# Gated attention and spatial mixer on one core: all four spatial chunks ahead of all sixteen output row tiles

## The chip, the cores and the metric

One core of a Trainium2 chip runs the whole kernel. The metric is the device time in microseconds (us). TensorE (PE) multiplies matrices into eight banks of PSUM, VectorE (DVE) and ScalarE (ACT) work on tiles of SBUF and read the banks, GpSimd (POOL) does almost nothing here, and SyncE (SP) issues most of the DMA transfers, in the order in which they are written; some are issued by ACT's queue. An engine works through its own queue in order.

## The reference

`x` is 2048 x 1024, bf16. The result is `g*a + (1-g)*b` with a gate `g` for each row.

```python
g = sigmoid((x * gate_w).sum(-1))
# a: attention over 8 earlier positions, 2 apart, 32 heads of 32
q, k, v = split(x @ wqkv)
o = softmax(q . k[pos - 2w] * scale) . v[pos - 2w]
a = o @ wo
# b: gated mixer, Fh = 1792
z = gelu(x @ w_in)                       # 2048 x 3584
z1, z2 = z[:, :Fh], layernorm(z[:, Fh:])
u = z1 * (w_sp @ z2 + b_sp[:, None])     # w_sp is 2048 x 2048
b = u @ w_out                            # 1792 x 1024
```

## The kernel before

The 2048 positions make 16 row tiles of 128; the 1792 columns of `z2` make 14 tiles f. All of SBUF's working space is one tile, `arena`, cut by hand into regions (Z for `z2`, X for the transposed `x`, A for the attention, CD and EF for what comes and goes); a region is used again by a later stage. Instructions keep the order in which the code issues them (`manual_schedule`), each engine in its own queue; the tile framework adds the waits. `Beat` (from L207) is the planner: `beat.run` advances a clock by the matmuls issued, `beat.at(t, fn)` issues `fn` when the clock passes `t`, and the steps of the attention, which DVE does, are issued between the matmuls of the stages that PE is in. So where a DVE step lands among the others follows from planned times, and where DVE runs behind the plan, the queue just gets later.

The stages on PE, in order: the second half of `z` (L279), `wqkv` (L501), the rest of `z2` (L279), `z1` (L538), which goes to DRAM, and then the spatial product, `w_sp @ z2`, in four chunks of 512 positions.

- Chunks 0 and 1 (`g_chunk`, L552) are 14 x 16 matmuls each. ACT copies each bank out (L556), DVE adds the bias and multiplies by `z1` (L557, L558), into `z1c_slots`.
- `final_chunk(0)` and `final_chunk(1)` make the output rows 0 to 7: for each row and half of the columns 8 matmuls of attention times `wo` (`attn_mm`, L565) and 14 of `u` times `w_out` (`mixer_mm`, L581); ACT scales the one (L588), DVE joins the two (L589).
- Chunks 2 and 3 are one product of 2 x 2 blocks with seven products in place of eight (`seven_products(n)` for n = 0 to 6, L668, 56 matmuls each). It multiplies sums of tiles in fp16: sums of `z2` (`s_sum`, L655 to L661) and sums of the weights (`t_sums`, `t1` to `t4`). The rows of the weights are scaled by powers of two first: they are loaded in natural order (`natural`), summed (`row_sums`, `row_sums_fast`), scaled (`scale_rows`), written to DRAM and loaded again transposed (`load_wsp`). In `seven_products` two banks are added to after they have been read: the last product adds to a bank that L708 (`TT(gsb, pb, e5)`) must have read.
- `late_chunks` makes the output rows 8 to 15 in four pairs. Each pair's mixer is again seven products of seven matmuls (`late_mix`, L828) with sums of `u` (`u_scale` L792, `u_sum` L799 to L805) and of `w_out` (`w_scale` L770, `w_sum` L775 to L781). The powers of two for `w_out` and `u` come from `w_largest` (L755), `u_sums` (L787, on ACT) and `whole_power`: small DVE steps with a transpose and a broadcast on PE between them (L740, L743). Between the last `seven_products` and the first pair stand attention products (`attn_pair(0)` and four halves, L810) and the sums for the pair.

`w_out` is loaded into X as soon as chunk 0 begins (L980). `wo` is loaded into A in two parts (`load_wo`, L417, five and three of its eight tiles; four transfers each), the first at the end of the attention's q and k. Its destination is strided by four partitions:

```python
dst = bass.AP(tensor=wo_sb.tensor, offset=wo_sb.offset + h * pitch + k0 * D,
              ap=[[pitch * HG, DH], [D, k1 - k0], [1, D]])
```

Of the kernel before, what the change touches and what calls it, by code (L numbers as in the profile page):

```python
# [10 lines left out]
F32 = mybir.dt.float32  # L11
# [4 lines left out]
P = 128  # L16
# [39 lines left out]
def kernel(  # L56
# [72 lines left out]
    w_max = sm.tile([P, 4], F32, name="w_max")  # L129
# [6 lines left out]
    u_up = sm.tile([P, 1], I32, name="u_up")  # L136
    back = sm.tile([P, 1], I32, name="back")
# [10 lines left out]
    w_out_sb = reg(X_OFF, NF * D).rearrange("p (f n) -> p f n", f=NF)  # L148
# [5 lines left out]
    wo_sb = reg(A_OFF, KT * D).rearrange("p (k n) -> p k n", k=KT)  # L154
    oT_slots = [reg(A_OFF + 8192 + r * 1024, 1024).rearrange("p (k t) -> p k t", k=KT) for r in range(3)]
    ob_slots = [reg(A_OFF + 11264 + r * 1024, 1024) for r in range(3)]
    asb_slots = [reg(A_OFF + 14336 + r * 1024, 1024).bitcast(F32) for r in range(2)]
# [9 lines left out]
                 reg(EF_OFF, 8192).rearrange("p (i a t) -> p i a t", i=16, a=4)]  # L167
# [5 lines left out]
    nat_slots = [reg(off, S) for off in (X_OFF + NF * D, A_OFF + 16384, A_OFF + 18432, X_OFF + NF * D)]  # L173
    nat_slots += [reg(CD_OFF + k * S, S) for k in range(4)]

    def half16(off, n):
        return reg(off, n * 512).bitcast(F16).rearrange("p (k t) -> p k t", k=n)

    sums = [reg(off, 1024).bitcast(F16).rearrange("p (k q) -> p k q", k=8)
            for off in (CD_OFF + 14336, A_OFF + 20480, EF_OFF + 8192, EF_OFF + 9216)]  # L180
    u_first = reg(EF_OFF + 10240, 2048).rearrange("p (h i q) -> p h i q", h=2, i=8)
    t1 = half16(CD_OFF + 8192, 8)
    t2 = half16(A_OFF + 16384, 8)
    t3 = half16(EF_OFF, 8)
    t4_parts = [half16(X_OFF + NF * D, 4), half16(CD_OFF + 12288, 4)]

    w_sums = reg(Z_OFF, 16 * FH).bitcast(F16).rearrange("p (f i n) -> p f i n", f=NF, i=4)
    late_asb = [reg(CD_OFF + r * 1024, 1024).bitcast(F32) for r in range(8)]
    late_oT = {a: oT_slots[a % 3] for a in (8, 9, 10)}
    for r, a in enumerate((11, 12, 13, 14)):  # L190
        late_oT[a] = reg(CD_OFF + 8192 + r * 1024, 1024).rearrange("p (k t) -> p k t", k=KT)
    late_oT[15] = late_oT[8]
    late_ob = ob_slots + [reg(A_OFF + 14336, 1024)]
    late_e5 = [reg(A_OFF + 16384 + r * 1024, 1024).bitcast(F32) for r in range(2)]
    late_sums = [[reg(EF_OFF + (4 * r + k) * 896, 896).bitcast(F16).rearrange("p (k q) -> p k q", k=7)
                  for k in range(4)] for r in range(2)]
# [179 lines left out]
    def attention_steps(t):  # L376
        beat.at(t - 8.0, lambda: load_qk(0))
        beat.at(t - 7.9, lambda: load_v(0))
        for g in range(NG):
# [3 lines left out]
            if g + 1 < NG:  # L383
                beat.at(t + 1.0, lambda g=g: load_qk(g + 1))
            else:
                beat.at(t + 1.0, lambda: load_wo(0, 5))
# [21 lines left out]
        beat.at(t + 1.5, lambda: load_wo(5, KT))  # L408
        for a in range(3):
            beat.at(t + 8.0, lambda a=a: load_oT(a))  # L410

    def load_wo(k0, k1):
        pitch = wo_sb.ap[0][0]
        for h in range(HG):
            dst = bass.AP(tensor=wo_sb.tensor, offset=wo_sb.offset + h * pitch + k0 * D,
                          ap=[[pitch * HG, DH], [D, k1 - k0], [1, D]])
            sync.dma_start(dst, wo_v[k0:k1, h, :, :].rearrange("g d n -> d g n"))  # L417

    def load_oT(a):
        sync.dma_start_transpose(oT_slots[a % 3], o_d[a * P:(a + 1) * P, :])  # L420
# [26 lines left out]
    def load_wsp(c, aa):  # L447
        src = wsp_v[4 * c + aa] if c < 2 else wsp_d[4 * (c - 2) + aa]
        sync.dma_start_transpose(wsp_slots[c % 2][:, :, aa, :], src)
# [78 lines left out]

    for f in range(NF):
# [16 lines left out]
    def g_chunk(c):  # L546
        wsp = wsp_slots[c % 2]
# [14 lines left out]
    def attn_mm(a, n0, nw):  # L562
        psa = psum.tile([P, 512], F32, name="psa", tag="ps")
        for kt in range(KT):
            nc.tensor.matmul(psa[:, 0:nw], oT_slots[a % 3][:, kt, :], wo_sb[:, kt, n0:n0 + nw],  # L565
                             start=(kt == 0), stop=(kt == KT - 1))
        beat.run(KT * nw)
        return psa

    def u_tile(f, a):  # L570
        if a < 8:
            return z1c_slots[a // 4][:, f, a % 4 * P:(a % 4 + 1) * P]
        return u_late(f)[:, a - 8, :]

    def u_late(f):
        return u_first[:, f // 7] if f % 7 == 0 else z2[:, f - 1, 0:8, :]

    def mixer_mm(a, n0, nw):
        psb = psum.tile([P, 512], F32, name="psb", tag="ps")
        for f in range(NF):  # L580
            nc.tensor.matmul(psb[:, 0:nw], u_tile(f, a), w_out_sb[:, f, n0:n0 + nw],  # L581
                             start=(f == 0), stop=(f == NF - 1))
        beat.run(NF * nw)
        return psb

    def combine(a, n0, nw, slot, psa, psb):
        asb = asb_slots[slot][:, 0:nw]
        nc.scalar.activation(asb, psa[:, 0:nw], ACT.Copy, scale=g_s[:, a:a + 1])  # L588
        nc.vector.scalar_tensor_tensor(ob_slots[a % 3][:, n0:n0 + nw], psb[:, 0:nw], omg[:, a:a + 1], asb,  # L589
                                       ALU.mult, ALU.add)  # L590
# [8 lines left out]
    def row_sums_fast(r):  # L599
        nc.vector.tensor_reduce(l1[:, r, 0:1], nat_slots[r], AX.X, ALU.add, apply_absolute_value=True)  # L600

# [5 lines left out]
    def row_powers(r0, r1, parts):  # L607
        v = nc.vector
        sl = slice(r0, r1)
        v.tensor_reduce(row[:, sl], l1[:, sl, 0:parts], AX.X, ALU.add)  # L610
# [26 lines left out]
    b_lo = wsp_slots[0].rearrange("p i a t -> p i (a t)")  # L637
    b_hi = wsp_slots[1].rearrange("p i a t -> p i (a t)")

    def t_sums(k):  # L640
        if k == 0:
            TT(t1, b_hi[:, 0:8], b_lo[:, 0:8], ALU.subtract)
        elif k == 1:
            TT(t2, b_hi[:, 8:16], t1, ALU.subtract)
        elif k == 2:
            TT(t3, b_hi[:, 8:16], b_hi[:, 0:8], ALU.subtract)
        else:
            h = 4 * (k - 3)
            TT(t4_parts[k - 3], b_lo[:, 8 + h:12 + h], t2[:, h:h + 4], ALU.subtract)
# [29 lines left out]
    def seven_products(n):  # L679
# [5 lines left out]
        e5 = asb_slots[n % 2]  # L685
# [7 lines left out]
        if more:  # L693
            s_sum(n + 1, 0)
        product(pb, sums[1], lambda k: t2[:, k], False)
# [8 lines left out]
        if n:  # L704
            w_scale(n - 1)
# [4 lines left out]
        if n:  # L710
            w_sum(n - 1, 0)
            w_sum(n - 1, 1)
# [6 lines left out]
        if n:  # L719
            w_sum(n - 1, 2)  # L720
            w_sum(n - 1, 3)
        product(pb, z2[:, fb, 8:16, :], lambda k: t4_parts[k // 4][:, k % 4], False)
# [5 lines left out]
        g_out(fb, 2, gsb)  # L728
        beat.run(56 * 512)

    def whole_power(src, up1):
# [18 lines left out]
        v.tensor_scalar(omg[:, 8:16], omg[:, 8:16], back[:].bitcast(F32), None, ALU.mult)  # L750
        yield

    def w_largest(k):
        f0, f1 = (0, 4, 8, 11, 14)[k:k + 2]
        nc.vector.tensor_reduce(w_max[:, k:k + 1], w_out_sb[:, f0:f1, :].rearrange("p f n -> p (f n)"), AX.X, ALU.max,  # L755
                                apply_absolute_value=True)
        if k == 3:
            nc.vector.tensor_reduce(top[:], w_max[:], AX.X, ALU.max)

    def w_tiles(j):  # L760
        f = (j + 1) % 7
# [3 lines left out]
    def w_t(j, k):  # L765
        return w_sums[:, j + 7 * (k // 2), 2 + k % 2, :]

    def w_scale(j):
        for f in ((j + 1) % 7, (j + 1) % 7 + 7):
            nc.vector.tensor_scalar(w_out_sb[:, f, :], w_out_sb[:, f, :], w_up[:].bitcast(F32), None, ALU.mult)  # L770

    def w_sum(j, k):
        b11, b12, b21, b22 = w_tiles(j)
        if k == 0:
            TT(w_t(j, 0), b12, b11, ALU.subtract)  # L775
        elif k == 1:
            TT(w_t(j, 1), b22, w_t(j, 0), ALU.subtract)
        elif k == 2:
            TT(w_t(j, 2), b22, b12, ALU.subtract)
        else:  # L780
            TT(w_t(j, 3), b21, w_t(j, 1), ALU.subtract)  # L781
# [7 lines left out]

    def u_scale(q):  # L790
        v = z2[:, :, 2 * q:2 * q + 2, :]
        nc.vector.tensor_scalar(v, v, u_up[:].bitcast(F32), None, ALU.mult)  # L792

    def u_sum(q, k):
        s = late_sums[q % 2]
        a11, a12 = z2[:, 0:7, 2 * q, :], z2[:, 7:14, 2 * q, :]
        a21, a22 = z2[:, 0:7, 2 * q + 1, :], z2[:, 7:14, 2 * q + 1, :]
# [236 lines left out]
```

## Time and profile before

| | |
|---|---|
| median of 3 runs | 701.32 us (701.2 to 702.38) |
| the profiled execution | 701.97 us, of which the span from first to last instruction is 700.2 us |
| PE busy | 691.3 us, 99% |
| DVE busy | 510.6 us, 73% |
| ACT busy | 306.0 us, 44% |
| POOL busy | 14.0 us, 2% |
| mean granted PE clock | 0.999 |
| HBM read, written | 51.91 MB, 32.57 MB |
| chunks 0 and 1 on PE | 366.6 to 463.5 us of the span |
| rows 0 to 7 | 463.5 to 541.7 us |
| `seven_products` | 541.7 to 626.3 us |
| rows 8 to 15 | 626.3 us to the last matmul's end at 696.5 us |

The stages' bounds are where the chain of waits goes from one line to the next. A matmul's record is longer than the time from one matmul to the next, since they are pipelined: 379 ns against 0.2158 us (768 matmuls of L501 follow each other in 165.76 us). A group of lines names engine, line and operation, what it writes and reads, then busy time and mean, then idle time ahead of it and what ended that.

### The profile page before, as it was taken

What the parts mean: (1) busy time and instruction counts of PE and PEld (TensorE: products, weight loads), DVE (VectorE), ACT (ScalarE), POOL (GpSimd) and SP (SyncE); (2) the same over time, 40 slices, a digit from 0 to 9 for tenths busy, and PEclk for the clock granted to TensorE, in tenths of its full rate; (3) what the DMA queues carried; (4) which work ended last, traced back from release to release, by engine and by line L of the source; (5) the groups of instructions that cost most, each with busy time, mean ns of one, the idle gap of its engine ahead of it and who ended that gap; (6) DMA issues with size and microseconds to landing.
All of it is one profiled execution on the core that took longest, in us unless ns stands there. A gap on an engine that the chain in (4) does not pass through costs nothing.

```text
span 700.2 us, 8520 instructions
## 1 busy us (share of the span) xinstructions
PE 691.3 (99%) x3232; PEld 355.6 (51%) x3281; DVE 510.6 (73%) x596; ACT 306.0 (44%) x576; POOL 14.0 (2%) x23
## 2 busy tenths in 40 slices
PE   8999999999999999999999999999999999999998
PEld 4466666666665554444444444444444444444443
DVE  0000398999999999999999999943496578677452
ACT  4444544435359887344351228533311254554211
POOL 1000000000000211000000000000000000000000
PEclk9999999999999999999999999999999999999999
DMA  9994974976465120994348973199852401130010
GB/s 225 188 192 91 263 170 126 237 175 178 125 168 183 57 102 28 216 315 137 105 147 233 367 233 136 61 294 204 197 131 61 122 30 46 45 62 16 30 61 30
DMA packets 182968, 101.29 MB, mean 145 GB/s; under 512 B 145808, under 2 KB 171408, under 8 KB 182672
## 3 DMA queue, kind: packets, MB, share of 16 engines
q1 hardware_dynamic: 180624, 92.37, 50.0%
q10 hardware_dynamic: 2304, 8.39, 3.3%
q8 instruction: 25, 0.41, 0.2%
q14 instruction: 15, 0.12, 0.1%
HBM read 51.91 MB, written 32.57 MB: 121 GB/s over the span
## 4 chain that ended last, share of the span: by engine, by line
PE 97%; DMA 2%; issue 0%; SPq 0%; DVE 0%; DVEq 0%
PE ps L501 24%; PE ps L552 14%; PE ps L538 14%; PE ps L279 14%; PE ps L668 12%; PE psb L581 7%; PE ps L828 6%; PE psa L810 4%; PE psa L565 3%; DMA arena<-in_B_w_in_dram 1%; DMA arena<-o_d 1%; SPq L459 0%; SPq L457 0%; PE po L743 0%; DVE arena L900 0%
## 5 line engine op out<-in xcount | busy, mean ns | idle before, releaser
L501 PE MATMUL ps<-arena 128*128 128x512 bf16 x768 | 165.9, 379 | 0.0
L501 PEld LDWEIGHTS <-arena 128*128 128x128 bf16 x768 | 110.7, 144 | 55.1
L323 DVE TENSOR_TENSOR arena<-arena 128x8192 bf16<-128x8192 bf16 x16 | 70.8, 4423 | 51.9 <-DMA arena<-k_d 51.6
L279 PE MATMUL ps<-arena 128*128 128x512 bf16 (+1 forms) x501 | 97.5, 353 | 1.7 <-DMA arena<-in_B_w_in_dram 1.1
L552 PE MATMUL ps<-arena 128*128 128x512 bf16 x439 | 96.6, 379 | 0.5
L538 PE MATMUL ps<-arena 128*128 128x512 bf16 x439 | 96.4, 379 | 0.5
L504 ACT CAST arena<-ps 128x512 bf16<-128x512 f32 x96 | 55.7, 587 | 93.2 <-PE ps L501 86.4
L668 PE MATMUL ps<-arena 128*128 128x512 f16 (+1 forms) x385 | 84.4, 379 | 0.4
L326 DVE TENSOR_TENSOR arena<-arena 128x4096 bf16<-128x4096 bf16 (+1 forms) x64 | 77.5, 1210 | 1.9
L279 PEld LDWEIGHTS <-arena 128*128 128x128 bf16 x512 | 50.1, 98 | 48.7 <-issue 2.1
L356 DVE TENSOR_TENSOR arena<-arena,att_A 128x8192 bf16<-128x8192 bf16 x16 | 70.7, 4421 | 0.2
L538 PEld LDWEIGHTS <-arena 128*128 128x128 bf16 x448 | 43.7, 98 | 52.8
L552 PEld LDWEIGHTS <-arena 128*128 128x128 bf16 x448 | 43.6, 98 | 52.8
L668 PEld LDWEIGHTS <-arena 128*128 128x128 bf16 (+1 forms) x392 | 38.3, 98 | 46.3
L540 ACT ACTIVATE arena<-ps 128x512 bf16<-128x512 f32 x56 | 32.3, 597 | 52.0 <-PE ps L538 39.6
L581 PE MATMUL psb<-arena 128*128 128x512 bf16 x220 | 50.0, 379 | 0.3
L284 ACT ACTIVATE arena<-ps 128x512 bf16<-128x512 f32 (+1 forms) x64 | 34.3, 538 | 25.7 <-PE ps L279 25.6
L828 PE MATMUL ps<-arena 128*128 128x512 f16 (+1 forms) x193 | 42.5, 379 | 0.2
L556 ACT CAST arena<-ps 128x512 bf16<-128x512 f32 x28 | 16.3, 582 | 51.7 <-PE ps L552 26.5
L362 DVE TENSOR_TENSOR arena<-arena 128x4096 bf16<-128x4096 bf16 x16 | 36.6, 2290 | 0.4
L588 ACT ACTIVATE arena<-psa,g_s 128x512 f32<-128x512 f32 x16 | 10.9, 686 | 58.3 <-PE psa L565 47.1
L581 PEld LDWEIGHTS <-arena 128*128 128x128 bf16 x224 | 21.7, 98 | 26.3 <-issue 0.2
(142 smaller groups left out, 573.9 us busy)
## 6 DMA issues: line engine op xcount, KB each, us to landing
arena<-k_d SPq DMA_DIRECT2D x8, 960.0 KB, 7.2
arena<-v_d SPq DMA_DIRECT2D x8, 960.0 KB, 5.3
z_d<-arena SPq DMA_DIRECT2D x14, 512.0 KB, 3.7
arena<-in_A_wqkv_dram SPq DMA_DIRECT2D x24, 256.0 KB, 4.4
arena<-in_B_w_in_dram SPq DMA_DIRECT2D x4, 1024.0 KB, 6.0
q_d<-arena SPq DMA_DIRECT2D x32, 128.0 KB, 2.3
k_d<-arena SPq DMA_DIRECT2D x32, 128.0 KB, 2.3
v_d<-arena SPq DMA_DIRECT2D x32, 128.0 KB, 2.4
```

Of the source, the lines that this page charges most:

```text
L279: nc.tensor.matmul(ps[:, 0:N], xT[:, kt, i * P:(i + 1) * P], w2[:, kt, ZC * c:ZC * c + N], start=(kt == 0), stop=(kt == KT - 1))
L323: TT(prod.rearrange("p (w j c) -> p w j c", w=W, j=8, c=C), in0, in1, ALU.mult)
L326: return lambda: TT(pv[:, :, 0:half], pv[:, :, 0:half], pv[:, :, half:2 * half], ALU.add)
L356: TT(prod.rearrange("p (w j d h) -> p w j d h", w=W, j=8, d=DH, h=HG), in0, in1, ALU.mult)
L362: return [(4.4, mul), (2.3, lambda: TT(p3[:, 0:4, :], p3[:, 0:4, :], p3[:, 4:8, :], ALU.add)), (1.2, lambda: TT(p3[:, 0:2, :], p3[:, 0:2, ...
L501: nc.tensor.matmul(ps[:].rearrange("p (t c) -> p t c", t=4), lhsT, wgt[:, :, kt, :], start=(kt == 0), stop=(kt == KT - 1))
L504: nc.scalar.copy(st[:, j % 4, :], ps[:])
L538: nc.tensor.matmul(ps[:], w1[:, kt, (f % 4) * P:(f % 4 + 1) * P], xT[:, kt, 512 * c:512 * (c + 1)], start=(kt == 0), stop=(kt == KT - 1))
L552: nc.tensor.matmul(ps[:], z2[:, f, i, :], wsp[:, i, :, :].rearrange("p a t -> p (a t)"), start=(i == 0), stop=(i == 15))
L581: nc.tensor.matmul(psb[:, 0:nw], u_tile(f, a), w_out_sb[:, f, n0:n0 + nw], start=(f == 0), stop=(f == NF - 1))
L668: nc.tensor.matmul(dst[:], lhs[:, k, :], rhs(k), start=first and k == 0, stop=k == 7, skip_group_check=not first)
L828: nc.tensor.matmul(dst[:], lhs(j), rhs(j), start=first and j == 0, stop=j == 6, skip_group_check=not first)
```

## The change

Chunks 0 and 1 are followed at once by `seven_products`; then all sixteen rows are made in eight pairs. Rows 0 to 7 now use the seven products too.

- `mix_pair(q)` takes the place of `late_mix`, and `attn_pair(q)` follows each `mix_pair`; `attn_mm`, `mixer_mm`, `combine`, `final_chunk`, `late_chunks` and the attention halves ahead of the first pair go. For the first four pairs `u` lies in `z1c_slots` and has a power of its own (`v_sum`, `v_up`), so there is a third `whole_power`.
- All eight row tiles of the weights are loaded by ACT's queue ahead of chunk 0, and summed and scaled (all sums on ACT) at planned times in chunks 0 and 1; `t_sums(0)`, `t_sums(1)` and the first `s_sum`s are issued at the end of chunk 1, `t_sums(2)` and `(3)` in n = 0, since `t2` and `t4` lie where chunk 1's weights were.
- The size of `w_out` is read beforehand: seven loads of two tiles (512 KB each) during `z1`, each summed by ACT. `w_out` itself is loaded in n = 1, into the attention's region A.
- `extra(n, place)` issues, at six places of each n, what goes beside the products: `w_scale` and `w_sum` for one tile in n = 3 and 5 and for two in n = 4 and 6 (before: one tile in each n from 1 on), the power for the first rows in n = 5 and 6, the load of `wo` (one part now, 512 KB in each of four transfers, into CD, where chunk 2's weights were) and the first pair's sums in n = 6.
- The rows of the attention's result are loaded (`load_oT`) into four slots, the first four after n = 6.

```diff
-    w_out_sb = reg(X_OFF, NF * D).rearrange("p (f n) -> p f n", f=NF)
+    w_out_sb = reg(A_OFF + 6144, NF * D).rearrange("p (f n) -> p f n", f=NF)
...
-    wo_sb = reg(A_OFF, KT * D).rearrange("p (k n) -> p k n", k=KT)
+    wo_sb = reg(CD_OFF, KT * D).rearrange("p (k n) -> p k n", k=KT)
...
+    u_first = reg(A_OFF, 2048).rearrange("p (h i q) -> p h i q", h=2, i=8)
+    e5_slots = [reg(A_OFF + 2048 + r * 1024, 1024).bitcast(F32) for r in range(2)]
+    t1 = half16(X_OFF + 8192, 8)
+    t2 = half16(EF_OFF, 8)
+    t3 = half16(X_OFF, 8)
+    t4 = half16(EF_OFF + 4096, 8)
...
+    def load_wo():
         pitch = wo_sb.ap[0][0]
         for h in range(HG):
+            dst = bass.AP(tensor=wo_sb.tensor, offset=wo_sb.offset + h * pitch, ap=[[pitch * HG, DH], [D, KT], [1, D]])
+            sync.dma_start(dst, wo_v[:, h, :, :].rearrange("g d n -> d g n"))
...
+    wout_v = B_w_out.rearrange("(f p) n -> p f n", p=P)
+    for k in range(7):
+        slot = look_slots[k % 2]
+        beat.at(beat.now + 4.0 + 11.0 * k, lambda k=k, slot=slot: sync.dma_start(
+            slot.rearrange("p (f n) -> p f n", f=2), wout_v[:, 2 * k:2 * k + 2, :]))
+        beat.at(beat.now + 14.0 + 11.0 * k, lambda k=k, slot=slot: nc.scalar.activation(
+            look_out, slot, ACT.Abs, accum_out=w_l1[:, k:k + 1]))
...
-    def seven_products(n):
+    def seven_products(n, extra):
...
+        extra(n, 0)
         pa = bank()
         product(pa, z2[:, fa, 0:8, :], lambda k: b_lo[:, k], True)
         pb = bank()
         nc.scalar.copy(pb[:], pa[:])
         pe = bank()
         product(pe, sums[0], lambda k: t1[:, k], True)
         nc.scalar.copy(e5, pe[:])
         if more:
             s_sum(n + 1, 0)
+        extra(n, 1)
         product(pb, sums[1], lambda k: t2[:, k], False)
...
         g_out(fa, 2, gsb)
-        if n:
-            w_scale(n - 1)
+        extra(n, 2)
         product(pb, sums[2], lambda k: t3[:, k], False)
         gsb = next_gsb()
         TT(gsb, pb[:], e5, ALU.add)
         g_out(fb, 3, gsb)
...
+        extra(n, 3)
         product(pc, sums[3], lambda k: b_hi[:, 8 + k], False)
...
         TT(gsb, pc[:], e5, ALU.add)
         g_out(fa, 3, gsb)
...
+        extra(n, 4)
...
+    def mix_pair(q):
+        a, b = 2 * q, 2 * q + 1
+        s = row_pair_sums[q % 2]
...
+        product7(pa, u_rows(q, 0, 0), lambda j: w_tiles(f_of(q, j))[0], True)
+        pb = bank()
+        nc.scalar.copy(pb[:], pa[:])
+        pe = bank()
+        product7(pe, s[0], lambda j: w_t(f_of(q, j), 0), True)
+        for r in (1, 0):
+            act(mix_slot(a + r, 512), pe[:], ACT.Copy, scale=og[r])
+        product7(pb, s[1], lambda j: w_t(f_of(q, j), 1), False)
...
+    def attn_pair(q):
+        for r in (2 * q, 2 * q + 1):
...
+                mix = mix_slot(r, 512 * (n0 // 512))[:, n0 % 512:n0 % 512 + nw]
+                nc.vector.scalar_tensor_tensor(ob[:, n0:n0 + nw], psa[:, 0:nw], g_s[:, r:r + 1], mix, ALU.mult, ALU.add)
...
+            if r + 4 < 16:
+                load_oT(r + 4)
+    w_sets = {3: (0,), 4: (1, 2), 5: (3,), 6: (4, 5)}
...
+    def extra(n, place):
+        if place == 0 and n == 0:
+            t_sums(2)
+        if place == 1 and n == 0:
+            t_sums(3)
+        if place == 0 and n == 1:
+            sync.dma_start(w_out_sb, wout_v)
+        for f in w_sets.get(n, ()):
+            if place == 2:
+                w_scale(f)
+            elif place in (3, 4):
+                w_sum(f, 2 * place - 6)
+                w_sum(f, 2 * place - 5)
+        if place == 2 and n < 5:
+            for f in range(3 * n, min(14, 3 * n + 3)):
+                v_sum(1, f)
+        if n == 5 and place == 5:
+            nc.vector.tensor_reduce(top[:], v_l1[:], AX.X, ALU.max)
+            powers["v"] = whole_power(top[:], v_up, slice(0, 8))
+            next(powers["v"])
+            nc.scalar.copy(z2[:, 13, 0:8, :], u_first[:, 1])
+        if n == 6:
+            if place in (1, 2):
+                next(powers["v"])
+            elif place == 3:
+                load_wo()
+            elif place == 4:
+                u_scale(0)
+                for k in range(4):
+                    u_sum(0, k)
     load_z1c(0)
+    t0 = beat.now
+    for r in range(8):
+        natural(r)
...
+    for r in range(4):
+        beat.at(t0 + 9.0 + 4.0 * r, lambda r=r: row_sums(r))
+        beat.at(t0 + 33.3 + 2.7 * r, lambda r=r: scale_rows(r))
+        beat.at(t0 + 50.0 + 3.5 * r, lambda r=r: load_wsp(2, r))
...
+        beat.at(t0 + 70.0 + 3.5 * r, lambda r=r: load_wsp(3, r))
...
+    for k in range(2):
+        beat.at(t0 + 86.0 + 2.5 * k, lambda k=k: t_sums(k))
+    for k in range(4):
+        beat.at(t0 + 91.0 + 0.8 * k, lambda k=k: s_sum(0, k))
...
     g_chunk(0)
     g_chunk(1)
-    final_chunk(0)
-    final_chunk(1)
+    for n in range(7):
+        seven_products(n, extra)
     beat.flush(1e9)
...
+    for a in range(4):
+        load_oT(a)
+    w_scale(6)
+    for k in range(4):
+        w_sum(6, k)
+    u_sums(6)
...
+    for q in range(8):
...
+        if q + 1 < 8:
+            u_scale(q + 1)
+            for k in range(4):
+                u_sum(q + 1, k)
+        mix_pair(q)
+        attn_pair(q)
```

More of the change, by code (lines that the diff above doesn't have):

```diff
@@ L136 @@
     u_up = sm.tile([P, 1], I32, name="u_up")
+    v_up = sm.tile([P, 1], I32, name="v_up")
     back = sm.tile([P, 1], I32, name="back")
@@ L990 @@
+    w_steps = whole_power(top[:], w_up, slice(0, 16))
+    for k in range(3):
+        beat.at(t0 + 6.0 + 14.0 * k, lambda: next(w_steps))
+    g_chunk(0)
     g_chunk(1)
[L991 to L992 removed]
+    for n in range(7):
+        seven_products(n, extra)
     beat.flush(1e9)
[L994 to L1000 removed]
```

359 lines of the change are left out of this document (100 added, 259 removed).

## The prediction

> **What bounds the kernel now.** I read the shares of the chain of waits first, then busy time by stage, the order of instructions on DVE and SP's queue, and last the single transfers. The chain:
>
> ```profile
> PE 97%; DMA 2%; issue 0%; SPq 0%; DVE 0%; DVEq 0%
> ```
>
> So PE sets the end: fewer matmuls are worth their full time, and any hole in PE costs its length. DVE stands close behind (PE's busy us in the second column group, then PEld, DVE, ACT):
>
> ```profile
> 366.60:415.00 48.40, 48.19 (x222) 21.80 (x225) 47.18 (x51) 10.14 (x17) 0.00 (x0) 1.00 0.86 268
> 415.00:463.50 48.50, 48.24 (x221) 21.93 (x226) 41.85 (x58) 31.33 (x60) 0.00 (x0) 1.00 0.43 146
> 463.50:541.70 78.20, 76.55 (x349) 34.35 (x355) 47.23 (x56) 17.16 (x21) 0.00 (x0) 1.00 0.72 172
> 602.15:614.24 12.09, 12.04 (x57) 5.47 (x56) 9.23 (x22) 5.68 (x13) 0.00 (x0) 1.00 0.16 45
> ```
>
> DVE is full in chunks 0 and 1 (attention). The stage the change removes, 463.5 to 541.7, is the one where it has room. In one n (the last line, n = 5) it needs 9.2 of 12.1 us. In order of time, DVE at the end of the attention and in n = 5:
>
> ```profile
> 454.82 0.68 DVE L359 TENSOR_TENSOR arena<-arena 128x1024 bf16<-128x1024 bf16 x1
> 455.43 0.42 DVE L557 TENSOR_TENSOR arena<-arena 128x512 bf16<-128x512 bf16 x1
> ...
> 609.73 0.42 DVE L671 TENSOR_TENSOR arena<-arena 128x512 bf16<-128x512 bf16 x1 [2.58 <-ACT arena L700]
> ...
> 611.32 0.68 DVE L708 TENSOR_TENSOR arena<-ps,arena 128x512 bf16<-128x512 f32 x1
> ...
> 618.21 0.42 DVE L673 TENSOR_TENSOR arena<-arena 128x512 bf16<-128x512 bf16 x1
> ```
>
> The attention ends at 455.5, 8 us ahead of chunk 1's end. n = 5 begins at 602.15; DVE starts on it 7.6 us in, reads the bank that the last product adds to (L708) at +9.2, and ends at +16.5, 4.4 us into n = 6.
>
> **The change, part by part.** All sums go against the profiled execution, 701.97 us (span 700.2); the median is 0.65 below it.
>
> (1) Matmuls. L581 had 8 rows x 28 = 224; four pairs have 4 x 49 = 196. 28 x 0.2158 us = 6.04 gone. PE's one wait for a transfer of o_d in that stage (1.3 us) goes with it. A third power adds L740 and L743, 0.15 + 0.32. Together **-6.9**. The built program has 52 fewer rows on PE, 28 pairs of load and matmul less two new ones, so the products are what the change says.
>
> (2) Chunk 1 into n = 0. Rows 0 to 7 stood between `t_sums` and their use; now nothing does. On DVE, ahead of the attention's end, come the power of w_out (12 small steps at 0.19, 2.4 us) and a second `row_powers` with its `back` (11 steps, 2.0): the attention ends at 459.8. The built order is then: f = 10's two steps (0.8), t1 2.28, f = 11 0.8, t3 2.28, f = 12 0.8, four `s_sum`s (L655 to L661) 2.65, f = 13 0.8, then t2 2.28, which must follow chunk 1's end: 472.5. PE ends chunk 1 at 464.1 and wants t2 two products (3.45) later, 467.6. **+4.9**. If DVE absorbs the small steps in its idle ahead of f = 11 and 12 (2.86 and 2.80), 0.6 remains; if chunk 0's `z1` comes late (below), 7.3.
>
> (3) n = 4 has two tiles to prepare: two `w_scale`s more (0.8) and four `w_sum`s (1.45). In the trace sums[1] for the next n is ready at 605.03, and n = 5's third product starts at 605.6; 2.25 later makes **+1.7** (0 to 2.3).
>
> (4) n = 5 ends on DVE 4.4 us into n = 6, and then come five small steps of the power (0.95), for which PE's transpose, now after n = 6's second product (3.45), waits until 5.4: 1.95. In n = 6, after the 0.8 of f = 6, two more `w_scale`s and seven steps of the power (1.15) stand ahead of L708's successor, which ends at 14.0; the last product waits for it, 1.2 more than its own time, and ends at 15.8 instead of 12.55. **+3.25** (0 to 3.5).
>
> (5) `load_wo`. In the built program its first transfer waits for exactly that DVE step (14.0), and the next step of that kind, `TT(gsb, pc, e5)`, waits for all four transfers to land, though `wo` and e5 lie apart. It is so in before: L588 there waits for all four of the second part, though its tile lies outside `wo`; there they had landed by about 471, before its bank was ready at 483. Behind the waiting step stand, on DVE, g_out (0.85), four `w_sum`s, `u_scale(0)`, four `u_sum`s, the last `g_out`, `w_scale(6)`, `w_sum(6)`: all that pair 0 needs. The price, from SP's queue and the transfers:
>
> ```profile
> 410.26 2.65 SPq L417 DMA_DIRECT2D arena<-in_A_wo_dram  x4
> ```
>
> ```profile
> arena<-in_A_wo_dram SPq DMA_DIRECT2D x4, 320.0 KB, 3.5
> arena<-in_A_wo_dram SPq DMA_DIRECT2D x4, 192.0 KB, 8.8
> ```
>
> Four of 320 KB took 6.8 us from the first issue to the last landing, by the issue times and those to landing. Four of 512 KB: 6.8 at least; 10.9 if all of it scales. The 192 KB ones, among 5 MB of others, took 15. Now little else moves; I take 9.0. So w_o is there at 23.1; L717's like and g_out 1.6, four `w_sum`s 1.4, `u_scale` (L792) 1.18: pair 0 starts at 27.3, PE having stood since 15.8. **+11.5** (9.3 to 17.5). Then `u_sum`s 2.27, g_out 0.8 and `w_scale(6)` 0.45 lead to 30.8, and pair 0's seventh matmul, ready at 28.6, waits for it; ACT's `u_sums(6)` stand ahead of the copy that the third product needs. **+2.3** (0 to 4).
>
> (6) PE after standing 11.5 us. The only such place in the trace is the start, where the same 128x512 matmuls are longer:
>
> ```profile
> L97 PE MATMUL pw<-const-bfloat16-1.0 x7: 312/631/632, 0.8 to 3.3; 128*128 128x512 bf16 x6, 128*128 128x128 bf16 x1
> ```
>
> 631 ns against 379 later (the first of L279 at 5.1 us are still 632, those at 7.1 us 377), while the clock's column reads 1.00. Pair 0's first six have a wait behind them that takes this up; the seventh and the seven of the next product lose about 0.2 each: **+1.5** (0 to 2.5). [...]
>
> (7) At nothing: ACT's more work, 7 looks of 2.2, 12 `row_sums` activations and 28 `v_sum`s of 0.82 (48 us in all, against the 19 of L588 and L819 that go), beside an ACT that is busy 44%; eight banks (28 us of chunk work) cover its lateness. SP's seven looks fall in `z1`, where its queue waits 22 us at a time for ACT. `load_oT`, 1.3 us of issue and 4.5 to landing, has 25 us ahead of its first use. In the pairs DVE needs 1.15 + 2.3 + 6 x 0.75 = 8 of 17.5 us. POOL has nothing new. Without these covers: each costs its own length, a few us.
>
> Sum: -6.9 + 4.9 + 1.7 + 3.25 + 11.5 + 2.3 + 1.5 = +18.2: 720.2 for a profiled execution, **719.5** for the median.
>
> **The rivals.** A: `load_wo` doesn't gate; DVE's queue alone does. `TT(gsb, pc, e5)` then follows its predecessors at 16.2, pair 0 starts at 20.3, 4.5 after PE is ready; with (6) small, -6.9 + 4.9 + 1.7 + 3.25 + 4.5 + 2.3 = +9.8, 711.1. For it: the tiles don't overlap. Against: the wait is in the program as built.
>
> B, the other side: DVE keeps up, since it has 2.6 to 3.2 us idle in each n and the few us of arrears in (2) to (5) dissolve, and `wo` lands within them; only (1) stays: 694.4. The point is where all holes together are under 6.9 us. For it: DVE busy 73% overall. Against: its order is fixed, and in (4) and (5) the needed steps stand last, behind the wait.
>
> C: loads collide. Eight row loads (4.2 MB) now go ahead of chunk 0's `z1` (1.8 MB, 7.1 us to landing alone); at the 347 GB/s of that stretch both take 17 us, to 384.7, where DVE wants `z1` at 382.3, with 2.4 us more in (2); and `wo` takes its 15 us, 6 more in (5): 728.
>
> D: without (6), the clock's part, all else as forecast: 718.0. [...]
>
> **How the numbers follow.** Forecast with 715 to 724 around it, D within: 0.63 (of that D a quarter). A: 0.13. C: 0.15. B: 0.04. A change within 0.2% (holes of 5.5 to 8.3 us), about what a measurement of this kernel can tell from no change: 0.03. What is left lies between A and the forecast. The range, 710 to 727, takes A in and most of C. Faster 0.04, same 0.03, slower 0.93.
>
> **What would show it.** In the profile after: a hole in PE of about 11 us ahead of the pairs' first product, ended by DVE's `u_scale(0)`, and on DVE a wait for `in_A_wo` of 7 us; a hole of about 5 us after chunk 1 that t2 ends; 1 to 2 us in n = 4 to 6; matmuls of some 630 ns after the hole; 196 matmuls fewer on the old L581's account replaced as in (1). Wrong it would be if that DVE step doesn't wait for the transfers (A), or if DVE is ahead of PE at n = 0 (then the small steps were absorbed).

## The result, and the profile after

The changed kernel takes 731.96 us (median of 4 runs, 730.51 to 732.09), the kernel before beside it 701.73 us (701.2 to 702.38): a ratio of 1.0426, 95% interval 1.0408 to 1.0444. The forecast was 719.5 us with a range of 710 to 727. The direction was right; the size was too small by 12.5 us and the range did not hold the time.

The profiled execution took 732.09 us (span 730.3), 30.1 more than that of before. PE is busy for 694.6 us, 95% of the span, where it had been 99%. The chain of waits is followed back only to 399 us here, so its shares add up to 44% and can't be set against the 97% of before; in the part that it covers, PE has three quarters and DVE most of the rest:

```profile
PE 33%; DVE 9%; DMA 2%; issue 0%; ACT 0%; SPq 0%; DVEq 0%
```

So PE no longer sets the end alone. What PE waited for (total us, times, longest):

```profile
PE ps L787 <- DVE arena L771: 11.4, 1, 11.4
PE pt L599 <- DVE b_up L594: 10.9, 1, 10.9
PE po L710 <- DVE top_b L706: 5.5, 2, 3.7
PE ps L639 <- DVE arena L680: 1.4, 2, 1.0
PE ps L639 <- DVE arena L628: 1.2, 1, 1.2
PE ps L787 <- DVE arena L732: 0.8, 1, 0.8
...
PE ps L639 <- DVE arena L617: 0.3, 1, 0.3
```

Every large wait is for a DVE result, and two of the names are small: `pt` and `po` are the banks of transposes of one small tile each. The forecast has no hole at either in chunks 0 and 1, and it has one of about 5 us at L617 (t2), where there are 0.3. By stage (us, PE's busy us, then PEld, DVE, ACT, POOL, and PE's granted clock third from the end):

```profile
365.77:414.20 48.43, 44.77 (x207) 19.97 (x207) 42.18 (x58) 24.66 (x62) 0.00 (x0) 1.00 0.85 259
414.20:479.62 65.42, 54.55 (x246) 24.22 (x245) 56.70 (x80) 39.32 (x69) 0.00 (x0) 0.92 0.72 172
479.62:570.60 90.98, 86.18 (x395) 38.09 (x393) 64.39 (x139) 48.27 (x114) 0.00 (x0) 1.00 0.23 76
570.60:582.02 11.42, 0.00 (x1) 0.01 (x1) 4.50 (x11) 2.87 (x6) 0.00 (x0) 0.60 1.00 265
```

Chunks 0 and 1 (the first two lines) take 113.85 us; in before they took 96.9 for the same matmuls. The seven products (third line) take 90.98, and then PE stands for 11.4 us ahead of pair 0. The holes themselves, in PE's order of time, with what ended them in brackets:

```profile
390.33 0.22 PE L710 MATMUL po<-ident,top_b 128*1 128x128 bf16 x1 [3.66 <-DVE top_b L706]
...
439.93 0.27 PE L599 MATMUL pt<-ident,b_up 128*8 128x128 bf16 x1 [10.87 <-DVE b_up L594]
...
582.02 2.74 PE L787 MATMUL ps<-arena 128*128 128x512 bf16 x6 [11.43 <-DVE arena L771]
585.60 11.58 PE L787 MATMUL ps<-arena 128*128 128x512 bf16 x43 [0.84 <-DVE arena L732]
597.02 7.07 PE L825 MATMUL psa<-arena 128*128 128x512 bf16 x32
```

The first two are the transposes of `whole_power` (for `w_out`) and of `scaled_biases`. Each takes a quarter of a microsecond, but PE works in the order of its queue, and the matmuls of the chunk that stand behind it could have run, as the experiments show: with the transpose of the biases planned later, its wait of 10.87 us is gone. In before the same two transposes stood in the stage of rows 0 to 7, where DVE had room (47.23 us busy of 78.20), and neither has a wait in brackets:

```profile
491.90 0.22 PE L628 MATMUL pt<-ident,b_up 128*8 128x128 bf16 x1
533.22 0.22 PE L740 MATMUL po<-ident,top_b 128*1 128x128 bf16 x1
```

In the changed kernel they stand in chunks 0 and 1, where DVE is full with the attention (98.88 us busy of 113.85), and DVE is late for two reasons. It has `row_powers(4, 8)`, its `back` and w's power to do as well; and it stood for 4.99 us for chunk 0's `z1`. With the eight row loads on ACT's queue, this load landed 10.1 us after its issue (7.1 in before), and the issue itself came 5.4 us later, because SP's queue waited 8.8 us for the last store of `z1` to land (2.5 in before). The issue in before:

```profile
370.38 0.33 SPq L452 DMA_DIRECT2D arena<-z_d  x1
```

And in the changed kernel, with two rows of DVE, its first step that reads `z1` and the one that writes `b_up`:

```profile
375.82 0.33 SPq L445 DMA_DIRECT2D arena<-z_d  x1
...
386.15 0.43 DVE L559 TENSOR_TENSOR arena<-arena 128x512 bf16<-128x512 bf16 x1 [4.99 <-DMA arena<-z_d]
...
439.71 0.16 DVE L594 TENSOR_TENSOR b_up<-b_in,up 128x8 bf16<-128x8 bf16 x1
```

`b_up` comes at 439.9. PE had reached its transpose at 429.07.

The third hole is the one that was forecast: DVE's L687 waits for `wo` (7 us forecast), and `u_scale(0)` ends the hole (11.5 forecast, 11.43 measured):

```profile
577.94 0.69 DVE L687 TENSOR_TENSOR arena<-ps,arena 128x512 bf16<-128x512 f32 x1 [6.78 <-DMA arena<-in_A_wo_dram]
```

### The profile page after: what moved, and what is told of

Same layout as the page of the kernel before. It is cut to its first block, busy times and chain, and to the rows that moved or that the text cites. A ratio compares the mean times of both kernels' runs of the same rounds, so it can differ in the third digit from the quotient of the medians.

```text
span 730.3 us, 8661 instructions
## 1 busy us (share of the span) xinstructions
PE 694.6 (95%) x3255; PEld 354.4 (49%) x3255; DVE 511.6 (70%) x629; ACT 347.8 (48%) x675; POOL 14.0 (2%) x23
## 5 line engine op out<-in xcount | busy, mean ns | idle before, releaser
L494 PEld LDWEIGHTS <-arena 128*128 128x128 bf16 x768 | 110.7, 144 | 55.1
L787 PE MATMUL ps<-arena 128*128 128x512 f16 (+1 forms) x392 | 89.5, 389 | 12.3 <-DVE arena L771 11.4
L497 ACT CAST arena<-ps 128x512 bf16<-128x512 f32 x96 | 55.8, 587 | 93.0 <-PE ps L494 87.4
L278 PE MATMUL ps<-arena 128*128 128x512 bf16 (+1 forms) x512 | 97.9, 354 | 0.2 <-DMA arena<-in_B_w_in_dram 0.2
L539 PE MATMUL ps<-arena 128*128 128x512 bf16 x448 | 96.9, 379 | 0.0
L639 PE MATMUL ps<-arena 128*128 128x512 bf16 (+1 forms) x392 | 85.8, 379 | 3.0 <-DVE arena L680 1.4
L278 PEld LDWEIGHTS <-arena 128*128 128x128 bf16 x512 | 50.2, 98 | 47.7 <-issue 1.0
L553 PEld LDWEIGHTS <-arena 128*128 128x128 bf16 x448 | 43.8, 99 | 53.5 <-issue 2.2
L539 PEld LDWEIGHTS <-arena 128*128 128x128 bf16 x448 | 43.8, 98 | 52.7
L787 PEld LDWEIGHTS <-arena 128*128 128x128 f16 (+1 forms) x392 | 38.9, 100 | 61.3 <-DVE arena L771 11.9
L825 PE MATMUL psa<-arena 128*128 128x512 bf16 (+2 forms) x264 | 56.6, 373 | 0.0
L828 DVE SCALAR_TENSOR_TENSOR arena<-psa,g_s,arena 128x512 bf16<-128x512 f32 (+2 forms) x33 | 24.2, 734 | 42.0 <-PE psa L825 42.0
L825 PEld LDWEIGHTS <-arena 128*128 128x128 bf16 x264 | 25.6, 98 | 30.0
```

Of the source, the lines that this page charges most:

```text
L278: nc.tensor.matmul(ps[:, 0:N], xT[:, kt, i * P:(i + 1) * P], w2[:, kt, ZC * c:ZC * c + N], start=(kt == 0), stop=(kt == KT - 1))
L494: nc.tensor.matmul(ps[:].rearrange("p (t c) -> p t c", t=4), lhsT, wgt[:, :, kt, :], start=(kt == 0), stop=(kt == KT - 1))
L497: nc.scalar.copy(st[:, j % 4, :], ps[:])
L539: nc.tensor.matmul(ps[:], w1[:, kt, (f % 4) * P:(f % 4 + 1) * P], xT[:, kt, 512 * c:512 * (c + 1)], start=(kt == 0), stop=(kt == KT - 1))
L553: nc.tensor.matmul(ps[:], z2[:, f, i, :], wsp[:, i, :, :].rearrange("p a t -> p (a t)"), start=(i == 0), stop=(i == 15))
L639: nc.tensor.matmul(dst[:], lhs[:, k, :], rhs(k), start=first and k == 0, stop=k == 7, skip_group_check=not first)
```

## The experiments

Theory Q: PE stands in its own queue for small DVE results, one hole after the other; when one goes, DVE's arrears show at the next place that needs DVE, t2 at n = 0 among them. The rivals: the holes are the whole cost and come back in full when taken away (R1), or they only move (R2), being due to the loads or to a DVE that is simply full.

**The transpose of the biases later.**

```diff
-    beat.at(t0 + 58.0, scaled_biases)
+    beat.at(t0 + 84.0, scaled_biases)
```

> Only the planned time of scaled_biases moves, from 58 to 84 us after the start of chunk 0, so that its transpose stands further back in PE's queue. Theory Q (PE stands in its own queue for a DVE result, and DVE's arrears show again at the next place that needs DVE): the hole of 10.87 us before L599 goes, with about 1.7 of half clock behind it, but DVE gains only the 5.85 us that it had stood waiting for PE, so t2 is late by about 7 us at n = 0 (0.34 in the changed kernel). Net about -5.5 us: 726.5. Rival R1 (the hole is the whole cost and nothing is behind it): -12.5, 719.5. Rival R2 (the hole is due to loads or to DVE alone and only moves): 0, 732.

721.78 us, ratio to before 1.0302 (1.0262 to 1.0341): 10.2 less, between Q and R1 and nearer to R1. One of the four runs took 727.08, at a mean granted clock of 0.983, the others 721.2 to 722.1 at 0.990 to 0.993. The waits, and below them rows of PE at t2 and at pair 0:

```profile
PE ps L787 <- DVE arena L771: 10.9, 1, 10.9
PE po L710 <- DVE top_b L706: 5.3, 2, 3.5
PE ps L639 <- DVE arena L617: 2.9, 1, 2.9
```

```profile
475.62 55.43 PE L639 MATMUL ps<-arena 128*128 128x512 f16 x256 [2.94 <-DVE arena L617]
...
573.50 2.74 PE L787 MATMUL ps<-arena 128*128 128x512 bf16 x6 [10.90 <-DVE arena L771]
577.08 9.44 PE L787 MATMUL ps<-arena 128*128 128x512 bf16 x43 [0.84 <-DVE arena L732]
```

The wait for `b_up` is gone and t2's is 2.9 instead of 0.3: as Q says, part of the gain was lost again at t2, but much less than the 7 us of Q's sum. I had counted 5.85 us of DVE's time spent waiting for PE; all such waits in the window were 7.4, and t2's product starts 7.96 earlier (475.62 against 483.58). The other 2.7 of the profiled run's 10.6 come at pair 0: half a microsecond of hole, and a half clock that ended 2.78 us into pair 0 instead of 7.95 (last section). R2 is out.

**The row loads later.**

```diff
-    for r in range(8):
+    for r in range(4):
         natural(r)
+    for r in range(4, 8):
+        beat.at(t0 + 14.0, lambda r=r: natural(r))
```

> Only four of the eight row loads move: rows 4 to 7 are issued 14 us after the start of chunk 0 and no longer ahead of chunk 0's z1. Theory: z1 of chunk 0 is on the chip about 5 us earlier, DVE's wait of 4.99 us for it goes, the hole of 3.66 us before L710 goes with it, and b_up comes 5 us earlier for a PE that comes 3.7 us earlier, so the hole before L599 is about 9.6: net -5 us, 727. Rival (the loads do not set it, DVE's attention steps do): z1 earlier but the holes as they were, 732. Other side: row sums of rows 4 to 7 are late and b_up with them: over 732.

728.7 us, ratio 1.0376 (1.0354 to 1.0399): 3.3 less.

```profile
387.03 0.22 PE L710 MATMUL po<-ident,top_b 128*1 128x128 bf16 x1 [0.33 <-DVE top_b L706]
...
436.60 0.27 PE L599 MATMUL pt<-ident,b_up 128*8 128x128 bf16 x1 [10.85 <-DVE b_up L594]
```

DVE's wait for `z1` fell from 4.99 to 1.6 us, not to nothing, and the gain is smaller than expected. `z1` landed 7.2 us after its issue again, but it was still issued at 375.4, 5 us later than in before, with four row loads still ahead of it. L710's first hole fell from 3.66 to 0.33 as expected; the hole before L599 is the same 10.85, where 9.6 was expected, since PE and DVE both came 3.3 us earlier. So the collision of the loads, rival C of the prediction, is there. The four rows moved are worth 3.3 us; what the other four cost, these runs don't show. It is not the collision alone that makes the largest hole.

**Both.** `scaled_biases` at 84 us and rows 4 to 7 later.

> Both edits: scaled_biases at 84 us and rows 4 to 7 loaded 14 us after the start of chunk 0. Theory Q: PE has no hole in chunks 0 and 1, and what is left is the one that the prediction forecast, t2 late at n = 0, of 5 to 6 us: chunks 0 and 1 take 97.4 instead of 113.85, n = 0 gets the hole, net about -10 us, 722. If step (2) of the prediction was right as to t2 itself, this hole is 4.9. Rival R1 (holes are given back in full): -16.5, 715.5. Rival R2 (they only move): 732.

721.5 us, ratio 1.0287 (1.0262 to 1.0313): 10.5 less, as Q expected. Chunks 0 and 1 take 97.73 us, from 365.71 to 463.44, with no hole, and this is the seam to n = 0:

```profile
463.44 1.89 PE L639 MATMUL ps<-arena 128*128 128x512 bf16 x8
466.75 1.90 PE L639 MATMUL ps<-arena 128*128 128x512 f16 x8 [1.41 <-DVE arena L626]
471.67 8.59 PE L639 MATMUL ps<-arena 128*128 128x512 f16 x39 [3.02 <-DVE arena L617]
```

1.41 and 3.02, with about 0.2 each to refill (the listed wait begins at the end of a matmul's record, and eight matmuls are recorded as 1.89 us where they take 8 x 0.2158): 4.8 us. That is the 4.9 of the prediction's step (2). So the step's sum was right for the event that it described; it left out what happens before it. Against the version with the biases alone, t2 is ready 4 us earlier (471.6, 475.6), yet the time is nearly the same (0.8 less in the profiled runs): there pair 0 took 12.86 us, here 15.51, by the clock, and the hole ahead of it is 0.5 longer.

**The hole before pair 0 filled with work.**

```diff
     beat.flush(1e9)
+    pw = bank()
+    for k in range(48):
+        nc.tensor.matmul(pw[:], ones[:, 0:P], ones[:, 0:512], start=True, stop=True)
```

> 48 matmuls of 128x512 on ones (10.4 us at 0.216) go into PE's queue between the last of the seven products and pair 0, so that PE is busy in the hole of 11.43 us that ends at u_scale(0). They add work whose result is unused. Theory (clock): pair 0 starts at the same time, its matmuls are at full speed, and pair 0 takes 12 to 13 us instead of 15.0: -2 to -3 us, 729.5. Rival (pair 0's extra 4.4 us are waits for DVE and ACT alone): 0, 732. Other side: PE or its power is worse off by the added work: over 732.

730.3 us, ratio 1.0402 (1.0381 to 1.0422): 1.7 less, under the 2 to 3 expected and not clear of the noise, for the interval overlaps that of the changed kernel (1.0408 to 1.0444) and the two profiled runs differ by 0.45. The trace says more than the time:

```profile
570.58 10.67 PE L906 MATMUL ps<-const-bfloat16-1.0 128*128 128x512 bf16 x48
582.00 1.47 PE L787 MATMUL ps<-arena 128*128 128x512 bf16 x6 [0.75 <-DVE arena L771]
585.58 11.13 PE L787 MATMUL ps<-arena 128*128 128x512 bf16 x43 [2.11 <-DVE arena L732]
```

The first six matmuls take 1.47 us instead of 2.74, but the seventh starts at the same time: it waits for `w_scale(6)`, 2.11 us now. So the prediction's 2.3 us for this wait were there in the changed kernel too, 1.27 of them covered by six slow matmuls. The 43 behind take 11.13: the granted clock was at 1.00 from 579.95 to 586.78, and behind this wait at 0.50 from there to 590.19. So the half clock before the seventh matmul was real (1.27 us on six matmuls), but filling one hole only moved the drop to the next.

**Where `wo` is loaded.** One kernel issues it behind the last step that reads e5, the other keeps e5 in 16 bits.

```diff
-            elif place == 3:
-                load_wo()
-            elif place == 4:
+            elif place == 4:
+                load_wo()
                 u_scale(0)
```

> Only load_wo moves, from place 3 to place 4 of n = 6, behind the last step that reads e5 (L687), so this step no longer waits for the landing. Theory W (the wait of L687 for w_o, 6.8 us, is what makes the hole before pair 0 longer than DVE's own order): pair 0 starts 6.8 us earlier, the hole shrinks from 11.43 to about 4.6, and up to 2 us of half clock go: 723 to 725. Rival A' (w_o itself, or DVE's order alone, sets pair 0's start): 730 to 732. Other side: w_o lands too late for the pairs' attention half and what writes beside it waits: over 732.

```diff
-    e5_slots = [reg(A_OFF + 2048 + r * 1024, 1024).bitcast(F32) for r in range(2)]
+    e5_slots = [reg(A_OFF + 2048 + r * 1024, 512).bitcast(F16) for r in range(2)]
```

> load_wo stays at place 3; e5, the two small tiles that L680 and L687 read, are kept in 16 bits with their columns inside the first half of their old place (the sum loses precision, nothing else changes). In this build neither L687 nor load_wo names the other any more, though the places of the data are the same as before. Theory W: as with load_wo at place 4, 723 to 725, so the wait guarded no data. Rival: 730 to 732.

725.64 us, ratio 1.0349 (1.033 to 1.0368), and 724.99 us, ratio 1.0338 (1.0322 to 1.0354): 6.3 and 7.0 less, the first 0.6 above the 723 to 725 expected. In both L687 waits for no transfer and the hole is the one expected (4.6):

```profile
PE ps L787 <- DVE arena L771: 4.6, 1, 4.6
```

Theory W holds: 6.8 us of the hole were the wait of a step whose data lay elsewhere (e5 in region A, `wo` in CD), and 4.6 are DVE's order. Why the built program has this wait, the runs don't show. The 2 us of clock were not saved; pair 0 takes 14.94 and 15.45, and with e5 in 16 bits, where it begins at 575.14, the granted clock was 0.62 from 572.90 to 576.31 and 0.50 from there to 583.14.

**The mixer's weights spread over more n.**

```diff
-    w_sets = {3: (0,), 4: (1, 2), 5: (3,), 6: (4, 5)}
+    w_sets = {2: (0, 1), 3: (2, 3), 4: (4,), 5: (5,), 6: (6,)}
...
-    w_scale(6)
-    for k in range(4):
-        w_sum(6, k)
...
-        if n == 5 and place == 5:
+        if n == 4 and place == 5:
             nc.vector.tensor_reduce(top[:], v_l1[:], AX.X, ALU.max)
```

> The mixer's weights are prepared one tile or two per n from n = 2 on (tiles 0 and 1 in n = 2, 2 and 3 in n = 3, then one each in n = 4, 5 and 6, none after the loop), and the power of v is taken one n earlier. Steps (3) and (4) of the prediction and the wait for w_scale(6) in pair 0 are to go: holes of 0.33, 1.24, 1.84, 1.04 and 0.84 us with 0.2 each to refill. If they stand in series with the wait for w_o: -5.5 us, 726.5. Rival (they are hidden, since pair 0 starts by the landing of w_o, whose issue does not move): 0 to -1, 731 to 732. Other side: two tiles in n = 2 and 3 make holes there: -5.5 + 2 x 1.7, 730.

729.52 us, ratio 1.0406 (1.0392 to 1.042): 2.4 less, near the "other side". The holes moved: L628 has two of 1.2 (n = 2 and 3, with two tiles each), and L710 keeps its 1.8, one n earlier. The seven products take 92.05 us, 1.1 more than in the changed kernel (90.98). They end at 570.66, where they ended before, only because they began 1.0 earlier: L710's first hole, in chunk 0, which this edit doesn't touch, was 2.7 in this run. What was gained lies at pair 0 (hole 10.2, and 13.0 us instead of 15.0). For the seven products R2 is right: DVE was late with two tiles in an n that also prepares the next one's sums, in the places that they have here.

**All of it, in three versions.** First all edits, with t2 ahead of t3 in DVE's order and `u_scale(0)` earlier.

> All together: scaled_biases late, rows 4 to 7 late, weights spread and v's power one n earlier, e5 in 16 bits; and t2 ahead of t3 and of two of the four s_sums in DVE's order, and u_scale(0) at the start of n = 6 with pair 0's sums at its end. If every hole is a wait for DVE in PE's queue, as the traces so far say, what is left is about 1 us for t2 and 0 to 2 before pair 0, and the 28 matmuls fewer show: 695 to 699. Rival (DVE is full and the holes only move into n = 2, 3 and 6): 700 to 706.

705.8 us, ratio 1.0065 (1.0052 to 1.0077): 26 less than the changed kernel, but above the 695 to 699 that Q gave and at the upper end of the rival's 700 to 706. Its waits of over a microsecond:

```profile
PE ps L639 <- DVE arena L628: 2.5, 2, 1.2
PE po L710 <- DVE top_b L706: 2.2, 2, 1.8
PE ps L787 <- ACT ps L801: 1.8, 1, 1.8
PE ps L639 <- DVE arena L680: 1.4, 4, 0.5
PE ps L639 <- DVE arena L617: 1.2, 1, 1.2
```

One of them is new, for ACT, whose copy stands behind `u_sums(6)`. The next version loads `w_out` at n = 0, prepares one tile per n, and puts `u_sums(6)` behind pair 0's copies:

```diff
-    w_sets = {2: (0, 1), 3: (2, 3), 4: (4,), 5: (5,), 6: (6,)}
+    w_sets = {1: (0,), 2: (1,), 3: (2,), 4: (3,), 5: (4,), 6: (5, 6)}
...
-    u_sums(6)
...
         mix_pair(q)
+        if q == 0:
+            u_sums(6)
```

> As the version with all edits, and further: w_out loaded at the start of n = 0 and one tile prepared in each n from 1 to 5 and two in n = 6 (which has no sums for a next n), v's power begun ahead of the last steps of n = 4 and u_scale(0) in n = 5, u_sums(6) and u's power behind pair 0's copies on ACT. Theory Q: the holes of 1.24 twice, 1.83, 1.81 and 0.74 us of the version before, all waits for a DVE or ACT result that stood behind work not yet needed, go with 0.2 each to refill; 1.2 for t2 stays: 705.8 - 7.5 = 698 to 699, below the kernel before. Rival (DVE has no room, so the holes move to other steps of the same n): 703 to 706.

702.79 us, ratio 1.0028 (1.0006 to 1.0051): above the 698 to 699 expected and next to the rival's 703. Of the five holes, L710's and the one for ACT went, L628's two fell from 1.24 each to 0.84 and 0.16, and pair 0's sums, behind two tiles in n = 6, came later and made the fifth 2.52 us instead of 0.74. The rival's direction was right for that one. The eleven runs spread from 701.0 (the profiled one) to 703.4, with one of 710.6, and the longer ones show the lower mean granted clock: 0.999 to 1.0 up to 702.1 us, 0.997 to 0.998 from 702.8 to 703.4, 0.990 at 710.6. That fits stretches at half clock that some runs meet and others don't; only the shortest run has a trace, so it is not shown. The last version puts the work where DVE's trace shows it idle, ahead of each n's first `g_out`, and moves two parts of w's power out of chunk 0:

```diff
         for f in w_sets.get(n, ()):
-            if place == 2:
+            if place == 1:
                 w_scale(f)
-            elif place in (3, 4):
-                w_sum(f, 2 * place - 6)
-                w_sum(f, 2 * place - 5)
+                w_sum(f, 0)
+            elif place in (2, 3, 4):
+                w_sum(f, place - 1)
...
+        if n == 1 and place in (0, 1):
+            next(w_steps)
+        if n == 6 and place in (3, 4):
+            u_sum(0, place - 3)
```

> As the last version, and the work of the mixer's weights is put where DVE's trace shows it idle in every n (2.8 us ahead of the first g_out, which waits for ACT), two of the three parts of w's power go from chunk 0 into n = 1, and pair 0's sums go in the order in which its products use them. Theory Q: the hole of 2.52 us at pair 0's second product falls to under 0.5, t2's of 1.22 goes, L628's and L680's of 2.1 halve: 4 to 5 us below the last version's 701.0 to 703.4, 697 to 699, below the kernel before. Rival (the medians of the last version lie above its profiled run for a reason that is not in these holes): 700 to 702.

696.89 us, ratio 0.9938 (0.9924 to 0.9951): faster than the kernel before, by 4.2 us, just under the 697 to 699 that Q gave. What PE waits for in it, from the second stage on, is the first, second and fourth of these lines:

```profile
PE ps L787 <- ACT ps L808: 1.0, 1, 1.0
PE ps L639 <- DVE arena L617: 0.9, 1, 0.9
PE pw L97 <- PEq L944: 0.8, 1, 0.8
PE ps L639 <- DVE arena L680: 0.5, 1, 0.5
```

It does the same matmuls as the changed kernel, and its DVE is busy for 509.5 us (511.6 there, 510.6 in before). So the 35 us between the two are a matter of order and of when loads are issued, with e5's precision the only difference in what is computed.

## Why the prediction was wrong, point by point

- **(1) Matmuls, -6.9: right as far as it can be seen.** With the holes gone, the kernel is 4.2 us under before with 2.4 us of waits left.
- **(2) Chunk 1 into n = 0, +4.9: this is the step that failed.** Chunks 0 and 1 with the seam cost 17.5 us more than in before (113.85 - 96.9, and 0.34 + 0.17 at t2). The prediction followed DVE to t2 and set PE's arrival at 464.1, as if PE went through chunks 0 and 1 unhindered. That is 0.6 us past before's 463.5, about what the two transposes and the broadcast that moved there take by themselves (0.15 to 0.3 us each); it did not ask who waits behind them. In the changed kernel PE came to n = 0 at 479.62, 15.5 later, and that is why t2's hole there was only 0.34: not because the small steps were absorbed, which the prediction named as the sign against it. PE stood 3.66 and 10.87 us, and half clock behind the second took 1.6 more (3.25 us at half rate). With both out of the way (the two edits together) t2's seam cost 4.8. The rule had been used in step (4), for v's transpose in n = 6, and not for the same code moved into a stage where DVE is full.
- **(3) n = 4's double set, +1.7: right**, 1.24 and 0.33 with the refill.
- **(4) Power and `w_scale` in n = 5 and 6, +3.25: right**, 1.84 and 1.04 with 0.2 each.
- **(5) `wo` gates, hole +11.5: right.** 11.43; L687 waited 6.78; the landing came 9.2 us after the first issue (9.0 taken). Rival A is out: with the wait gone the hole is 4.55, the 4.5 that A had. The 2.3 for `w_scale(6)` is 0.84 of wait and 1.27 of slow matmuls in its place.
- **(6) The clock, +1.5: right in kind, 2.1 by size** (43 matmuls in 11.58 us, 9.44 where the clock had come back). The term was my estimate from the start of before's trace (631 ns a matmul against 379). Rival D is out: half clock in mid-run is in the records (0.50 from 432.94 to 443.18 us and from 572.90 to 589.97).
- **Rival B** (DVE keeps up, 694.4) needed all holes under 6.9 us; it failed here, but the last experiment is near it, after the order was changed.
- **Rival C** (loads collide, 728) was there in its first half only: `z1` landed at about 385.9 (384.7 in the rival's sum) and DVE stood 4.99 us for it, where the rival had 2.4; moving half of the row loads brought 3.3 in time. `wo` did not take 15 us. That its total lay close to the measured one is luck.

The sum of what was measured is -6.9 + 17.5 + 1.9 + 3.2 + 11.6 + 2.3 + 2.1 = +31.7, against 30.1 in the profiled run. Of the rest, 0.64 is an earlier start of chunk 0 (365.77 against 366.41), and about 0.6 are the matmuls of w's power and of the biases (0.15, 0.32 and 0.15 from each start to the next), which came into chunks 0 and 1 from the stage that went and are counted in the 17.5. The last 0.3 is open.

## What to carry to other kernels

When a change moves code, list every instruction that it puts into the queue of the engine that sets the end, the quarter-microsecond transposes and broadcasts first, and ask for each when its operand is ready and what stands behind it: its price is the wait, not its length (here 10.87 us for a transpose of 0.27). A planned time is safe only in a stage where the producer has room. When holes stand in series for one producer, the gain of taking one away is what the producer catches up (here 7.96 of the 10.6 us by which PE came earlier to t2's place), and the next trace names what is left.

## What the runs showed of the hardware that I had not expected

PE's granted clock fell to half in mid-run and came back. The moments are worked out from its mean in stretches of 1 us (PE busy first, clock third from the end). In the changed kernel it was at 0.50 from 432.94 to 443.18 us and from 572.90 to 589.97, 10.24 and 17.07 us long:

```profile
432.00:433.00 1.00, 0.00 (x0) 0.00 (x0) 0.96 (x2) 0.57 (x2) 0.00 (x0) 0.97 0.91 296
433.00:434.00 1.00, 0.00 (x0) 0.00 (x0) 1.00 (x2) 0.00 (x0) 0.00 (x0) 0.50 1.24 193
...
442.00:443.00 1.00, 1.00 (x4) 0.30 (x2) 1.00 (x1) 0.00 (x0) 0.00 (x0) 0.50 0.16 39
443.00:444.00 1.00, 1.00 (x5) 0.45 (x4) 1.00 (x1) 0.00 (x0) 0.00 (x0) 0.91 0.79 169
...
572.00:573.00 1.00, 0.00 (x0) 0.00 (x0) 0.00 (x0) 0.78 (x3) 0.00 (x0) 0.95 1.05 397
573.00:574.00 1.00, 0.00 (x0) 0.00 (x0) 0.00 (x0) 0.00 (x0) 0.00 (x0) 0.50 1.13 289
...
588.00:589.00 1.00, 1.00 (x4) 0.34 (x3) 0.97 (x3) 0.00 (x0) 0.00 (x0) 0.50 0.00 0
589.00:590.00 1.00, 1.00 (x4) 0.42 (x3) 0.93 (x2) 0.79 (x2) 0.00 (x0) 0.52 0.00 0
590.00:591.00 1.00, 1.00 (x7) 0.42 (x5) 1.00 (x2) 0.47 (x1) 0.00 (x0) 1.00 0.00 0
```

With the biases late it was at 0.50 from 391.96 to 395.37 us and from 566.04 to 576.28, 3.41 and 10.24 us long:

```profile
391.00:392.00 1.00, 1.00 (x6) 0.43 (x5) 0.97 (x2) 0.97 (x3) 0.00 (x0) 0.98 1.13 159
392.00:393.00 1.00, 1.00 (x4) 0.37 (x3) 0.99 (x2) 0.94 (x4) 0.00 (x0) 0.50 1.26 284
...
394.00:395.00 1.00, 1.00 (x3) 0.29 (x2) 0.97 (x3) 0.20 (x1) 0.00 (x0) 0.50 1.07 217
395.00:396.00 1.00, 1.00 (x5) 0.44 (x4) 1.00 (x2) 0.00 (x0) 0.00 (x0) 0.81 1.99 367
...
566.00:567.00 1.00, 0.00 (x0) 0.00 (x0) 0.00 (x0) 0.00 (x0) 0.00 (x0) 0.52 1.02 377
567.00:568.00 1.00, 0.00 (x0) 0.00 (x0) 0.00 (x0) 0.00 (x0) 0.00 (x0) 0.50 1.03 389
...
575.00:576.00 1.00, 1.00 (x3) 0.30 (x2) 1.00 (x3) 0.00 (x0) 0.00 (x0) 0.50 0.00 0
576.00:577.00 1.00, 0.24 (x1) 0.00 (x0) 0.97 (x4) 0.29 (x1) 0.00 (x0) 0.86 0.00 0
577.00:578.00 1.00, 0.92 (x5) 0.44 (x5) 0.97 (x4) 0.97 (x3) 0.00 (x0) 1.00 0.00 0
```

In three of the four it fell while PE stood and came back some time after PE had gone on: 3.25 us after (439.93 to 443.18), 7.95 (582.02 to 589.97, with 0.84 of wait between) and 2.78 (573.50 to 576.28). In the fourth, at 391.96, it fell 1.40 us after the hole before L710 had ended.

The length of a hole alone did not decide it. L710's first hole, with the 64 matmuls behind it up to L713, in the changed kernel, with the biases late, and with the hole before pair 0 filled:

```profile
390.33 0.22 PE L710 MATMUL po<-ident,top_b 128*1 128x128 bf16 x1 [3.66 <-DVE top_b L706]
390.48 13.99 PE L553 MATMUL ps<-arena 128*128 128x512 bf16 x64
404.40 0.39 PE L713 MATMUL po<-top,const-bfloat16-1.0 1*128 1x512 bf16 x1
```

```profile
390.56 0.22 PE L710 MATMUL po<-ident,top_b 128*1 128x128 bf16 x1 [3.51 <-DVE top_b L706]
390.71 15.67 PE L553 MATMUL ps<-arena 128*128 128x512 bf16 x64
406.32 0.38 PE L713 MATMUL po<-top,const-bfloat16-1.0 1*128 1x512 bf16 x1
```

```profile
390.46 0.22 PE L710 MATMUL po<-ident,top_b 128*1 128x128 bf16 x1 [3.61 <-DVE top_b L706]
390.61 13.99 PE L553 MATMUL ps<-arena 128*128 128x512 bf16 x64
404.53 0.39 PE L713 MATMUL po<-top,const-bfloat16-1.0 1*128 1x512 bf16 x1
```

From the transpose's successor to L713 it is 13.92 us, 15.61 and 13.92: with the biases late the clock fell, in the changed kernel it read 1.00 all the while (386 to 400 us). So a hole of 3.5 to 3.7 us cost 1.7 us or nothing, and the hole before pair 0, of 11.43, 10.90 and 11.39 us, kept pair 0 at half clock for 7.95 us in the changed kernel, 2.78 with the biases late and 8.98 with both edits. What decides it, these runs don't show. As an estimate from these figures, each such hole has a chance of some 2 us more, and it makes 2.7 of the 4 us that the later row loads gained at t2 and lost again at pair 0.
